# Another cut of the tokens for a fused linear attention and gated MLP: nine tokens of a head per partition, pairs of heads in 64-row halves

## The chip, the cores and the metric

The kernel runs on one core of a Trainium2 chip. The metric is device microseconds of one execution; the time before is the median of three runs. The engines are TensorE (PE, with the weight loads as a row of their own, PEld), VectorE (DVE), ScalarE (ACT), GpSimd (POOL) and SyncE (SP), which here only issues DMAs and waits. PSUM has 8 banks of 512 float32 a partition; every matmul writes there.

## The reference

Inputs: `q`, `k`, `v` of shape (8 batches, 8 heads, 576 tokens, 64), `w_phi` (64 x 128), and for the MLP `w_val`, `w_out` (512 x 512) and `conv_w` (5 x 512), all float32.

```python
def phi(x):
    proj = np.einsum('bhsd,df->bhsf', x, w_phi)
    proj = proj - np.max(np.abs(proj), axis=-1, keepdims=True)
    return np.concatenate([np.exp(proj), np.exp(-proj)], axis=-1)
q_p, k_p = (phi(q), phi(k))
kv = np.einsum('bhsf,bhsd->bhfd', k_p, v)
z = np.sum(k_p, axis=2)
num = np.einsum('bhsf,bhfd->bhsd', q_p, kv)
den = np.einsum('bhsf,bhf->bhs', q_p, z)[..., None] + 1e-06
attn = num / den                      # heads side by side: x of (8, 576, 512)

gate_pre = sum over k of conv_w[k] * (x shifted down by 4 - k tokens, zeros ahead)
out = (sigmoid(gate_pre) * (x @ w_val)) @ w_out
```

So every token and head needs two projections to 128 features, the largest magnitude of each, and 256 exponentials for q and for k. The sum over tokens KV (with a column of ones for z) must be complete for a head before any of its outputs can be computed. The convolution looks at a token and the four before it.

## The kernel before

**Units.** The 576 tokens of a head are cut into 512 main tokens, four neighbours on each of 128 partitions, and a tail of 64. A main unit is one pair of heads of one batch (32 of them); a tail unit holds the tails of two batches, all heads (4). 36 units in all.

**One unit's steps**, by the names in the list and the lines of the profile:
- `T` (L331): four transposes each for k and q, 128x128, into one bank; `Tc` copies that bank to SBUF (L224 on DVE, L222 on ACT).
- `PK`, `PQA` (L342): projection of k and q with tokens on the output partitions, eight matmuls of 64 rows each, for the two halves of the rows into two banks. `mKa`, `mK`, `mQa`, `mQ` (L356) take the largest magnitude of each, one bank at a time.
- `E` (L382) and `K0` to `K3` (L388): exponentials on ACT. The maximum of k is not subtracted; its exponential scales v instead, in `V` (L408, on POOL), whose extra column (L412) carries the scale for z.
- `PQ` (L466): projection of q again, now with features on the partitions, two matmuls of 64 rows by 512 columns. `SH` (L476) subtracts the maximum in PSUM, with a broadcast column against a negated identity, eight matmuls of 128 rows and columns. `Qa`, `Q` (L484): exponentials, 512 elements at a time.
- `KV` (L445, L450): 16 matmuls of 128 rows for the main tokens and 4 for the tail; `KVM` copies the sums to SBUF (L224, L222). `NUM` (L509; L523 for tails), then `XN`: reciprocal (L534) and product (L536).
- `XP`: a DMA transpose issued by SP (L545, L548) puts the normalised tokens, channels on partitions, into `XT` (tails: `XH`).

**The MLP**, for each batch: `GA` (L604) computes the convolution with diagonal 64x64 weights, four tiles of the array at a time, in two calls of 32 matmuls with two banks each; `TH` (L612) the tanh; `VAa`, `VAb` (L617) the product with `w_val`; `GV` (L633) gate times value; `OUT` (L642) the product with `w_out`; `OE` (L649 on ACT, L651 on DVE) the evacuation with a factor of one half; `ST` (L663) the store. `GAt`, `THt`, `GVt`, `OUTt` (L673 to L712) do the same for the tails of two batches.

**Loads.** `LD` (L295) issues them, most from POOL, which converts float32 to bfloat16 on the way; a main load takes rows of 1,024 bytes, a tail's rows of 256.

**Order.** Nothing is scheduled at run time. The string `ORDER` lists every step with its PSUM bank (`@`) and, where there is a choice, its engine (`:D`, `:A`, `:P`); each engine and queue executes its own steps in the order of the list, and waits for semaphores. So a step that waits holds all that stands behind it on the same engine.

A matmul addresses a part of the array: 128 rows, or a half of 64, and the same for columns. Matmuls in different parts can overlap.

Of the kernel before, what the change touches and what calls it, by code (L numbers as in the profile page):

```python
# [2 lines left out]

# [7 lines left out]
ALU = mybir.AluOpType  # L11
# [9 lines left out]
SM = 512  # L21
ST = S - SM
E1 = D + 1
PL = 144
TL = 80
NG = B // 2
NU = 9 * NG


# [7 lines left out]
LD5 V2:P mKa4 K33 K04 KVM1:D NUM1@4 PQ3@6,3 SH3 mK4 XN1 LD11 K13 KV2@2 K24 LD31 PQA4@7,4 KVM2:D E3
mQa4 K14 mQ4 PQ0@1,5 K34 SH0 LD30 Qa3 Qa0 NUM2@6 PQ4@2,0 T5@4 T6@1 Q3 SH4 Q0 XN2 Qa4 E4 Tc5:D
Tc6:D PK5@7,6 mKa5 K05 PQA5@3,1 PK6@2,5 mQa5 Q4 LD13 K15 mK5 LD12 V3:P K25 KV3@3 mQ5 V4:P mKa6 K06
LC0 K35 KVM3:D E5 V5:P LD32 LD39 PQ5@0,1 TP0@7 mK6 Vb0:P NUM3@3 CW0 XP1 XN3 K16 XP2 T7@7 Tc7:D K26  # L40
SH5 Qa5 PQA6@6,2 mQa6 PK7@3,7 mKa7 KV4@4 PQA7@6,0 mQ6 mQa7 XP3 K36 T8@5 Tc8:D mK7 PQ6@2,6 Q5
KVM4:A SH6 K07 NUM4@4 mQ7 XN4 E6 PK8@0,1 K17 mKa8 Qa6 K27 T9@2 Tc9:D Q6 XP4 PQA8@3,5 V6:P PQ7@4,6
SH7 mQa8 LD15 mK8 K08 K37 PQA9@2,3 mQ8 mQa9 KV5@7 KVM5:D mQ9 T10@5 Tc10:D K18 PQ8@0,2 SH8 Qa7
PK9@4,7 mKa9 T11@3 E7 V7:P Q7 PK10@5,6 Tc11:D K28 mKa10 LD14 DG0:P Qa8 K38 KV6@3 Q8 K09 NUM5@0 mK9
KVM6:D NUM6@2 XN5 K010 mK10 KV7@0 K29 K110 XN6 K19 KVM7:D T12@5 PK11@1,4 mKa11 K210 HL0:P Tc12:D
XP6 LD16 K39 GA0@2 K310 mK11 K011 NUM7@6 VAa1@0 LD40 XN7 E8 VAb1 TH0 GV1 V8:P PK12@2,5 PQA10@3,6
K111 PQ9@1,7 SH9 VAa2@0 K211 mQa10 mKa12 LD19 VAa0@3 mK12 E9 LD17 K311 Qa9 VAb0 mQ10 KV8@4 KVM8:D
VAb2 GV0 PQA11@1,6 K012 V9:P Q9 mQa11 K212 PQ10@4,7 SH10 mQ11 K112 T13@3 Tc13:D NUM8@1 XN8 E10
# [59 lines left out]
def kernel(  # L110
# [653 lines left out]
```

## Time and profile before

| | |
|---|---|
| runs | 235.14, 232.63, 233.62 us; median 233.62 |
| profiled execution, first to last instruction | 232.5 us (the page gives no other time for it) |
| busy, PE / PEld | 205.8 us (89%) / 139.5 us (60%) |
| busy, DVE / ACT / POOL | 184.2 (79%) / 188.6 (81%) / 125.4 us (54%) |
| chain that ended last, by engine | PE 69%, ACT 11%, DMA 9%, DVE 5% |
| mean granted clock of TensorE | 0.972 |
| maxima L356 / exponentials L388 and L484, calls | 144 / 288 |

A line of groups reads: source line, engine, operation, output<-inputs with shapes, count, then busy time and the mean of one, then idle time of the engine before them. A line of the timeline begins with the start and the length in us, and ends with an idle time where the engine waited. A line of stages gives the window, its length, busy time and count of PE, PEld, DVE, ACT and POOL, the granted clock, and the DMA's share and rate. A PE duration holds some latency: the next matmul starts before it ends.

### The profile page before, as it was taken

How to read it: one execution, taken by the hardware profiler on the slowest of the kernel's cores; microseconds unless marked ns; L12 is line 12 of the kernel's file. 1: busy time of each engine (PE TensorE's matmuls, PEld its weight loads, DVE VectorE, ACT ScalarE, POOL GpSimd, SP SyncE). 2: the span in 40 equal slices, each digit the busy share in tenths (PEclk: the TensorE clock that was granted, in tenths of full speed). 3: DMA queues.
4: the chain of work that ended last, by engine and by line, in shares of the span. 5: the costliest groups of instructions: out<-in, count | busy, mean ns of one | idle time of the engine just before them, and what ended most of it. 6: DMA issues, size and time to landing. Idle time of an engine off the chain costs nothing.

```text
span 232.5 us, 8372 instructions
## 1 busy us (share of the span) xinstructions
PE 205.8 (89%) x3497; PEld 139.5 (60%) x3516; DVE 184.2 (79%) x335; ACT 188.6 (81%) x419; POOL 125.4 (54%) x142
## 2 busy tenths in 40 slices
PE   1286797888999989899999999999899999999991
PEld 1264675666666746567666766766476667564550
DVE  5559669999989979699999879897799788554451
ACT  3189869999997988599999979998899999934251
POOL 8909935999979437774919751564526241100000
PEclk9998579999999999999999999999999999999997
DMA  8997995979999942999994992499903928126195
GB/s 151 246 198 97 106 180 80 92 101 178 129 194 128 139 32 32 129 257 177 128 114 68 180 186 92 39 115 126 214 6 37 169 77 259 38 52 200 27 355 185
DMA packets 62002, 30.90 MB, mean 133 GB/s; under 512 B 33420, under 2 KB 59148, under 8 KB 61964
## 3 DMA queue, kind: packets, MB, share of 16 engines
q0 software_dynamic: 36144, 14.29, 58.2%
q1 hardware_dynamic: 25468, 15.78, 33.6%
q8 instruction: 27, 0.44, 0.8%
q10 hardware_dynamic: 352, 0.30, 0.4%
q14 instruction: 11, 0.09, 0.2%
HBM read 30.48 MB, written 9.44 MB: 172 GB/s over the span
## 4 chain that ended last, share of the span: by engine, by line
PE 69%; ACT 11%; DMA 9%; DVE 5%; issue 3%; SPq 1%; POOL 1%; POOLq 0%; DVEq 0%; ACTq 0%
PE PS L617 11%; PE PS L642 10%; PE PS L342 7%; PE PS L604 7%; PE PS L476 7%; PE PS L445 6%; PE PS L331 6%; DMA XT<-XN 6%; PE PS L509 5%; ACT QTIL L484 5%; ACT KTIL L388 3%; DMA kT<-in_k_dram 3%; PE PS L466 3%; PE PS L681 2%; DVE MQ L356 2%
## 5 line engine op out<-in xcount | busy, mean ns | idle before, releaser
L408 POOL TENSOR_TENSOR VT<-vN,E 128x1024 bf16<-128x1024 bf16 x27 | 51.5, 1907 | 60.4 <-issue 34.2
L388 ACT ACTIVATE KTIL<-PS 128x512 bf16<-128x512 f32 x128 | 76.7, 666 | 5.3 <-DVE MK L356 5.1
L484 ACT ACTIVATE QTIL<-PS 128x512 bf16<-128x512 f32 x128 | 71.0, 666 | 2.5 <-PE PS L476 1.1
L356 DVE TENSOR_REDUCE MK<-PS 128x4 f32<-128x512 f32 x72 | 47.9, 683 | 7.5 <-PE PS L342 7.2
L356 DVE TENSOR_REDUCE MQ<-PS 128x4 bf16<-128x512 f32 x72 | 47.4, 683 | 1.3 <-PE PS L342 1.2
L342 PE MATMUL PS<-W,T 64*128 64x128 bf16 x576 | 29.6, 227 | 5.8 <-DVE T L224 1.9
L617 PE MATMUL PS<-XT,WVAL 128*128 128x512 bf16 x128 | 33.8, 380 | 0.3 <-DMA XT<-XN 0.3
L342 PEld LDWEIGHTS <-T 64*128 64x128 bf16 x576 | 18.3, 98 | 21.8 <-issue 11.9
L642 PE MATMUL PS<-WOUT,GV 128*128 128x512 bf16 x111 | 29.9, 380 | 1.2 <-issue 0.5
L633 DVE SCALAR_TENSOR_TENSOR GV<-GATE,PS 128x512 bf16<-128x512 bf16 x32 | 21.6, 681 | 5.9 <-ACT GATE L612 3.1
L445 PE MATMUL PS<-VT,KTIL 128*128 128x65 bf16 x512 | 25.4, 198 | 0.8 <-DVE T L224 0.6
L536 DVE TENSOR_TENSOR XN<-PS,RCP 128x512 bf16<-128x512 f32 x36 | 24.9, 691 | 1.2
L445 PEld LDWEIGHTS <-KTIL 128*128 128x128 bf16 x512 | 22.8, 100 | 3.7 <-DVE T L224 0.8
L476 PE MATMUL PS<-nident,MQ 128*128 128x128 bf16 x288 | 23.9, 229 | 0.5 <-issue 0.5
L612 ACT ACTIVATE GATE<-PS 128x1024 bf16<-128x1024 f32 x16 | 16.7, 1044 | 8.8 <-PE PS L604 8.7
L476 PEld LDWEIGHTS <-MQ 128*128 128x128 bf16 x288 | 17.6, 102 | 9.5 <-issue 8.8
L224 DVE COPY T<-PS 128x1024 bf16<-128x1024 bf16 x31 | 21.1, 684 | 2.7 <-PE PS L331 2.3
L509 PEld LDWEIGHTS <-QTIL 128*128 128x128 bf16 x512 | 19.3, 99 | 5.5 <-DVE KVS L224 1.1
L509 PE MATMUL PS<-KVS,QTIL 128*128 128x65 bf16 x512 | 21.4, 196 | 1.3 <-DVE KVS L224 0.8
L450 PE MATMUL PS<-VZ,KTt 128*128 128x65 bf16 x128 | 21.9, 196 | 0.0
L604 PE MATMUL PS<-XT,DIAG 64*64 64x384 bf16 (+3 forms) x512 | 20.6, 299 | 1.0 <-issue 0.8
L642 PEld LDWEIGHTS <-GV 128*128 128x128 bf16 x128 | 11.3, 98 | 12.4 <-issue 0.6
(73 smaller groups left out, 304.1 us busy)
## 6 DMA issues: line engine op xcount, KB each, us to landing
out_dram<-OS SPq DMA_DIRECT2D x14, 512.0 KB, 3.8
kN<-in_k_dram POOLq DMA_DIRECT2D x7, 512.0 KB, 9.0
qN<-in_q_dram POOLq DMA_DIRECT2D x7, 512.0 KB, 8.4
vN<-in_v_dram POOLq DMA_DIRECT2D x7, 512.0 KB, 6.9
vF<-in_v_dram SPq DMA_DIRECT2D x2, 512.0 KB, 7.6
out_dram<-OSt SPq DMA_DIRECT2D x8, 128.0 KB, 2.4
out_dram<-OS SPq DMA_DIRECT2D x4, 256.0 KB, 2.9
qT<-in_q_dram POOLq DMA_DIRECT2D x8, 64.0 KB, 5.2
```

The costliest lines, as they stand in the source:

```text
L342: nc.tensor.matmul(PS[:, bank[rg], blk * P:(blk + 1) * P], u.T[r, i, blk, :], W2[r, :], start=True, stop=True,)
L356: nc.vector.tensor_reduce(dst, PS[:, bank, :].rearrange("p (b f) -> p b f", f=F), AX.X, ALU.max, apply_absolute_value=True,)
L388: nc.scalar.activation(u.KT[:, ft, rg, :, :].rearrange("p b f -> p (b f)"), PS[:, u.PK[rg], :], AF.Exp, scale=1.0 if ft == 0 else -1.0,)
L408: eng.tensor_tensor(dst[:, :, :, 0:D], x.unsqueeze(1).to_broadcast([n, 2, 8, D]), e.unsqueeze(3).to_broadcast([n, 2, 8, D]), ALU.mult,)
L445: nc.tensor.matmul(o, u.KT[:, ft, rg, h2 * 2 + j2, :], u.VT[:, ft, (h2 * 2 + j2) * 2 + rg, :], start=(c == 0), stop=False,)
L476: nc.tensor.matmul(PS[:, u.PQ[rg], blk * P:(blk + 1) * P], u.MQ[:, rg, blk:blk + 1].to_broadcast([P, P]), nident[:, :], start=False, stop= ...
L484: nc.scalar.activation(u.QT[:, ft, rg, :, :].rearrange("p b t -> p (b t)"), PS[:, u.PQ[rg], :], AF.Exp, scale=1.0 if ft == 0 else -1.0,)
L509: nc.tensor.matmul(ps[:, j2, x * E1:(x + 1) * E1], u.QT[:, ft, rg, h2 * 2 + j2, :], u.KVS[:, (ft * 2 + h2) * E1:(ft * 2 + h2 + 1) * E1], s ...
L536: nc.vector.tensor_tensor(u.XN[:, :, :, :], nv[:, :, :, 0:D], RCP[:, :, :].unsqueeze(3).to_broadcast([P, 2, 4, D]), ALU.mult,)
L604: nc.tensor.matmul(ps[c, par, j0 * P:j1 * P], DIAG[r, dt, 4 - dl, :], mv, start=(i == 0), stop=(i == len(parts) - 1), skip_group_check=True,)
L617: nc.tensor.matmul(PS[:, m.val[jt], :], WVAL[:, dt, jt * P:(jt + 1) * P], XTs[m.b % 2][:, dt, :, 16:PL], start=(dt == 0), stop=(dt == 3),)
L642: nc.tensor.matmul(PS[:, bank[0], :], m.GV[:, jt, j * P:(j + 1) * P], WOUT[:, jt, :], start=(jt == 0), stop=(jt == 3),)
```

## The change

The kernel is written anew around another cut of the tokens, with another list.

- A partition holds nine neighbouring tokens of one head; 64 partitions hold a head, 128 a pair. Plane n is the n-th token of every partition. A unit is a pair of heads with planes 0 to 7 (32 units); plane 8 of a batch's four pairs makes a "halo" unit, one per batch (8). In the list, units have plain names (`T5`, `KV5`), halos a trailing e (`Te1`, `PKe1`).
- The two heads of a pair lie on different halves of the partitions, so transposes, `SH` and `KV` become 64-row matmuls, one half for each head: 16, 16 and 36 a unit, where there were 8, 8 and 20. T's output and the KV sums take two banks each.
- `mQ` takes the maximum over two banks in one call; `Qp`, `Qm` are exponentials over two banks. K stays with one bank a call.
- `PQ` is split. Both halves of the rows write both banks, so `PQb` may start only when `PQa` has finished: `WQ` puts a nop on SP that waits for `PQa`'s last matmul, and `PQb`'s first matmul waits for that nop.
- Taps: 32x32 diagonal weights, 16 tiles of the array, 144 matmuls a batch into four banks; plane 8 of two batches is computed together by `GAe`, 80 matmuls, `VAe`, `OUTe`.
- `w_val` is loaded in its own order and rearranged by four POOL copies (`WC`); `w_out` in four loads.
- Loads take rows of 2,304 bytes. The second to fourth unit to be started belong to batch 1, whose k and q are loaded whole (`LQ1`, `LK1`).
- 28 of the 32 units reach `XT` by the DMA transpose on SP (`XC` without an engine), the last four, and the halos, by PE transposes. A store is two DMAs, for even and odd planes.
- Eight matmuls of zeros stand ahead of everything on PE.

```diff
-SM = 512
-ST = S - SM
+HP = H // 2
+NPL = 9
...
+    for i in range(NF):
+        nc.tensor.matmul(PS[:, 7, :], zero[:, 0:P], zero[:, :], start=True, stop=True)
...
     def op_T(i, bank):
         u = units[i]
-        u.Tps = PS[:, bank[0], :].bitcast(BF16).rearrange("p (i b t) -> p i b t", i=2, b=4)
+        u.Tps = half(bank[0], 256).bitcast(BF16)
         for n, name in enumerate(("k", "q")):
-            for blk in range(4):
-                nc.tensor.transpose(u.Tps[:, n, blk, :], col(u, name, blk), ident_bf[:, :])
+            for jj in range(4):
+                for h2 in range(2):
+                    r = row(h2)
+                    nc.tensor.transpose(
+                        u.Tps[:, h2, (n * 4 + jj) * 64:(n * 4 + jj) * 64 + 64],
+                        tok(name, u.b)[r, u.hp, jj * P:(jj + 1) * P], ident[r, r],
+                    )
 
     def op_Tc(i, eng):
         u = units[i]
-        u.T = ktp.tile([P, 2, 4, P], BF16, name="T")
-        copy(eng, u.T[:, :, :, :], u.Tps)
+        u.T = ktp.tile([P, 2, 4, 2, 64], BF16, name="T")
+        copy(
+            eng, u.T[:, :, :, :, :].rearrange("p n j h t -> p h (n j) t"),
+            u.Tps.rearrange("p h (x t) -> p h x t", t=64),
+        )
...
+    def op_mQ(i):
+        u = units[i]
+        u.MQ = maxp.tile([P, 2, 4], BF16, name="MQ")
+        absmax(u.MQ[:, :, :], half(u.PQA, 512).rearrange("p g (j f) -> p g j f", f=F))
...
+    def op_KV(i, bank):
+        u, t = units[i], halos[units[i].b]
+        u.KVps = half(bank[0], 2 * E1)
+        for ft in range(2):
+            for n in range(NPL):
+                for h2 in range(2):
+                    r = row(h2)
+                    if n < 8:
+                        kt, vt = u.KT[r, ft, n % 2, n // 2, :], u.VT[r, ft, n, :]
+                    else:
+                        kt, vt = t.KT[r, ft, u.hp % 2, u.hp // 2, :], t.VT[r, ft, u.hp, :]
+                    (nc.tensor.matmul(
+                        u.KVps[:, h2, ft * E1:(ft + 1) * E1], kt, vt,
+                        start=(n == 0), stop=(n == 8), skip_group_check=True,
+                    ))
...
+    def unswapped(proj, u):
+        u.last = [proj(u, g, 1) for g in range(2)][1]
...
+    def relay(u):
+        u.relay = nc.sync.nop()
+        behind(u.relay, u.last)
+
+    def swapped(proj, u):
+        behind([proj(u, g, 0) for g in range(2)][0], u.relay)
+
+    def featproj(u, g, swap):
+        h2 = g ^ swap
+        return nc.tensor.matmul(
+            PS[:, u.PQ + h2, :].rearrange("p (j g t) -> p g j t", g=2, t=64)[:, g, :, :],
+            W2[row(g), :], u.T[row(g), 1, :, h2, :],
+            start=True, stop=False, skip_group_check=True,
+        )
...
+    def submax(bank, cols):
+        for n, col in enumerate(cols):
+            for h2 in range(2):
+                r = row(h2)
+                nc.tensor.matmul(
+                    PS[:, bank + h2, n * 64:n * 64 + 64], col[r, :].to_broadcast([64, P]), nident[r, r],
+                    start=False, stop=True, skip_group_check=True,
+                )
...
+    def qexp(u, ft):
+        new_qt(u)
+        nc.scalar.activation(
+            u.QT[:, ft, :, :, :].rearrange("p h n t -> p h (n t)"), half(u.PQ, 512),
+            AF.Exp, scale=1.0 if ft == 0 else -1.0,
+        )
...
+    def taps(X, bank, rs, parts):
         for i, (dl, j0, j1) in enumerate(parts):
-            for dt, r, c, par in quarters(q2):
+            for dt in range(4):
+                for r in rs:
+                    rr = slice(32 * r, 32 * r + 32)
+                    g = PS[32 * dt:32 * dt + 32, bank[r // 2] + r % 2, j0 * 64:j1 * 64]
...
+                    nc.tensor.matmul(
+                        g, DIAG[rr, dt, 4 - dl, :], mv,
+                        start=(i == 0), stop=(i == len(parts) - 1), skip_group_check=True,
+                        tile_position=(32 * r, 32 * dt),
+                    )
```

Two lines of the new list, from the middle, and one from its end:

```
Tc15:D mKb14 XCe2:D KV13@0 Ka14 E14 OE1_1:D PQb13 SH13 PQA14@2 KVM13:A LV4 GA2@0,4 mQ14 NUM12@2 RCP12 V14:P
Qm13 Qp13 XN12 NUM13@6 THx2 PQa14@0 WQ14 T16@2 RCP13 PQb14 XN13 SH14 Tc16:D THy2 PK15@4,5 KV14@6 mKa15 XC12
...
OUT7_1 OE7_1:A STe2 ST6_3 VAe3@7 OUT7_2 OUTp7_3@2 THey3 OUT7_3 ST7_0 GVe3 OUTe3@3 OE7_2:A ST7_1 OEe3:A OE7_3:D
```

More of the change, by code (lines that the diff above doesn't have):

```diff
@@ L37 @@
[L37 to L42, printed above, removed]
@@ L456, in op_KVM @@
     def op_KVM(i, eng):
         u = units[i]
[L458 to L469 removed]
+        u.KVS = kvp.tile([P, 2, 2 * E1], BF16, name="KVS")
```

986 lines of the change are left out of this document (534 added, 452 removed), and 14 rows, old and new, of the table LOADS.

## The prediction

> **What bounds the kernel now.** I read the busy time by stage first, then short stretches of the timeline, where the distance from the start of one group to the start of the next gives what an operation occupies of its engine (a duration also holds latency that the next operation overlaps).
>
> ```profile
> 45.00:195.00 150.00, 143.51 (x2629) 98.44 (x2644) 134.24 (x245) 138.82 (x313) 92.01 (x98) 1.00 0.99 125
> 195.00:228.00 33.00, 32.01 (x446) 18.30 (x448) 17.25 (x33) 17.11 (x33) 2.10 (x2) 1.00 0.48 149
> 8.05 0.60 ACT L388 ACTIVATE KTIL<-PS 128x512 bf16<-128x512 f32 x1 [2.62 <-DVE MK L356]
> 203.26 1.13 ACT L484 ACTIVATE QTIL<-PS 128x512 bf16<-128x512 f32 x2
> 227.76 0.69 DVE OS L651
> ```
>
> The stage rows give PE, PEld, DVE, ACT and POOL in that order. From 45 to 195 us PE is busy 143.5 of 150 (96%), ACT 138.8, DVE 134.2: PE binds, with two engines close behind. From 195 to 228 PE is full and the others half idle: MLP work left over when attention has ended. ACT's exponentials run from 8.05 to 204.4; the last evacuation starts at 227.76 and ends at 228.5, and the store with the closing takes 4 more to 232.5. So time falls with PE work, but only until ACT or DVE binds.
>
> **PE's work, before and after.** What each block occupies:
>
> ```profile
> 103.06 1.29 PE L604 MATMUL PS<-XT,DIAG 64*64 64x512 bf16 x32
> 104.29 0.40 PE L342 MATMUL PS<-W,T 64*128 64x128 bf16 x8
> ...
> 105.29 0.29 PE L445 MATMUL PS<-VT,KTIL 128*128 128x65 bf16 x4
> ...
> 105.92 0.66 PE L509 MATMUL PS<-KVS,QTIL 128*128 128x65 bf16 x16
> 106.41 1.03 PE L617 MATMUL PS<-XT,WVAL 128*128 128x512 bf16 x4
> ...
> 109.61 0.40 PE L342 MATMUL PS<-W,T 64*128 64x128 bf16 x8
> 109.85 0.38 PE L466 MATMUL PS<-T,W 64*128 64x512 bf16 x2
> 110.06 0.39 PE L342 MATMUL PS<-W,T 64*128 64x128 bf16 x8
> 110.38 0.62 PE L476 MATMUL PS<-nident,MQ 128*128 128x128 bf16 x8
> 110.84 1.03 PE L617 MATMUL PS<-XT,WVAL 128*128 128x512 bf16 x4
> 111.70 0.29 PE L445 MATMUL PS<-VT,KTIL 128*128 128x65 bf16 x4
> ```
>
> A unit before: KV, 20 matmuls, 105.92-105.29 = 0.63; NUM 0.49; projections PK and PQA 0.24 each (109.61 to 109.85); PQ 0.21; the maximum subtraction SH 0.46 (8 of 128 columns), and the 8 transposes T, of the same shape, 0.45. L342 takes 0.32 where the next group has another tile shape, so a change of shape costs about 0.09. Taps GA: 1.23 with a change, 1.13 without, twice a batch; a VA block 0.86, and OUT, of the same shape, as much. Sums: 32 main units of 2.72 = 87.0; 4 tails of 2.1 = 8.5; MLP 8 x (2.26+3.44+3.44) = 73.1; the tails' MLP 4 x 2.3 = 9.2; 164 changes of shape (counted along the matmul rows) x 0.09 = 14.8. Together 193.
>
> After, T (16 matmuls), SH (16) and KV (36) have 64 rows and 64 or 65 columns, in alternating halves of the array, a form that this trace lacks. The nearest rows:
>
> ```profile
> 96.35 0.76 PE L673 MATMUL PS<-XH,DIAG 64*64 64x128 bf16 x40
> 97.05 1.07 PE L681 MATMUL PS<-XH,WVAL 128*128 128x128 bf16 x16
> 118.54 0.70 PE L523 MATMUL PS<-KVS,QTt 128*64 128x65 bf16 x32
> ```
>
> L673, four tiles at once: (0.70-0.09)/40 = 15 ns each. L523, two halves by columns, 65 wide: 0.70, less the 0.17 by which L509's 0.66 exceeds its 0.49, over 32 = 16 ns. L509, one tile, 65 wide: 0.49/16 = 31. So 15 to 31 ns; I take 16, since L342 (two row halves, 128 wide: 0.24/8 = 30 ns, half of L476's 57) shows row halves running side by side with full-width weights. Then T is 0.26 for 0.45, SH 0.26 for 0.46, KV 0.58 for 0.63: 0.44 less a unit, 14 in all; at 31 ns it would be 0.58 more a unit, 19 in all.
>
> The Trainium skill, "TensorE: Matmul & The Clock Gate", section "Back-to-back issue gap", speaks against this: a matmul of 1 to 64 columns still takes about 60 cycles, a floor of 25 ns. By that floor 68 matmuls would take 1.7 us a unit and 144 taps 3.6 us a batch, an estimate that undoes the gain. The 15 and 16 ns of L673 and L523 disagree, at least where neighbours use different tiles.
>
> The rest of PE: PK, PQA, PQ and NUM keep columns and concurrency, 1.18, so a unit is 2.28, x32 = 73.0. Eight halos of 1.1 (Te 0.26, PKe 0.24, PQe 0.11, SHe 0.13, NUMe 0.26, XPe 0.11) = 8.9. Four units' PE transposes XP at the end 0.9. Taps in 32x32 tiles, also unseen: 16 tiles at once halve the columns, 2.26 to 1.13, if the array limits; 144 x 15 ns = 2.2 if each costs L673's pace. I take 1.5, nearer the array's, since most of the 144 are long. MLP 8 x 8.4 = 67.0. The halos' MLP has 80 taps, 0.3 to 1.2, taken 0.7: 4 x 2.5 = 9.8. Changes of shape, counted in the new list, 158: 14.2. Together 174, from 166 to 219 with the bounds.
>
> **The relays.** In 40 places PQb now waits for an SP nop that itself waits for PQa's last matmul; all that stands behind PQb on PE waits along, and DVE and ACT for that.
>
> ```profile
> 5.30 0.61 PE L331 MATMUL PS<-ident_bf,qN 128*128 128x128 bf16 x4
> 5.94 0.69 DVE L224 COPY T<-PS 128x1024 bf16<-128x1024 bf16 x1
> 6.69 1.04 PE L342 MATMUL PS<-W,T 64*128 64x128 bf16 x16 [0.79 <-DVE T L224]
> L545 SPq DMA_TRANSPOSE XT<-XN x32: 1189/1210/2460, 28.4 to 208.9; - x32
> ```
>
> PE's end at 5.91 starts DVE at 5.94, DVE's end at 6.63 starts PE at 6.69: hops of 0.03 and 0.06. The latency of a 256-column matmul is about 0.28 (L466's 0.38 less half of the 0.21 it occupies). PE must then cover 0.37 less the 0.11 that PQa occupies, 0.26. The list puts a PE block of 0.23 to 0.9 between in most places, some 0.12 in four, nothing in four: about 3 us. On SP a relay also queues behind crossbar transposes, which wait for XN and hold SP 1.21 us each; seven stand within six entries ahead of a relay, four of these well covered: 2 us. I take 5 (no gain is possible; 25 at 0.6 a relay). PE after: 179, which is 14 less.
>
> **ACT and DVE.**
>
> ```profile
> 46.17 1.89 ACT L388 ACTIVATE KTIL<-PS 128x512 bf16<-128x512 f32 x3
> 47.60 1.43 ACT L484 ACTIVATE QTIL<-PS 128x512 bf16<-128x512 f32 x2
> 48.56 0.66 ACT L382 ACTIVATE E<-MK 128x8 f32<-128x8 f32 x2
> 48.76 1.44 ACT L484 ACTIVATE QTIL<-PS 128x512 bf16<-128x512 f32 x2
> 200.65 1.02 ACT L612 ACTIVATE GATE<-PS 128x1024 bf16<-128x1024 f32 x1 [0.58 <-PE PS L604]
> 201.56 1.08 ACT L484 ACTIVATE QTIL<-PS 128x512 bf16<-128x512 f32 x2
> 203.00 0.42 ACT L222 ACTIVATE KVS<-PS 128x260 bf16<-128x260 f32 x1
> 60.07 1.28 DVE L356 TENSOR_REDUCE MK<-PS 128x4 f32<-128x512 f32 x2
> 61.27 0.68 DVE L356 TENSOR_REDUCE MQ<-PS 128x4 bf16<-128x512 f32 x1
> 62.16 0.43 DVE L224 CAST KVS<-PS 128x260 bf16<-128x260 f32 x1 [0.22 <-PE PS L450]
> 62.51 0.68 DVE L633 SCALAR_TENSOR_TENSOR GV<-GATE,PS 128x512 bf16<-128x512 bf16 x1
> 64.30 0.68 DVE L224 COPY T<-PS 128x1024 bf16<-128x1024 bf16 x1
> 64.90 0.20 DVE L534 RECIPROCAL RCP<-PS 128x8 f32<-128x8 f32 x1
> 65.14 0.69 DVE L536 TENSOR_TENSOR XN<-PS,RCP 128x512 bf16<-128x512 f32 x1
> ```
>
> ACT: 512 elements occupy 1.43/3 = 0.477, a pair E 0.20, 1024 elements 0.91, a KVS copy 0.26. Up to its last exponential it does 288 exponentials (137), 36 E pairs (7), 13 tanh and 5 T copies (16), and 24 smaller ones (12): 172 in the 196 from 8.05, 88%. The change: pairing Q's exponentials over two banks saves 0.04 each, 64 times (-2.8); four T copies go (-3.7); eight KVS copies come (+2.1); four output evacuations, a tanh and eight halo E pairs more fall before the last exponential (+4). It stays at 172.
>
> DVE: a 512 maximum or T copy occupies 0.60, a KVS copy 0.35, RCP with XN 0.24 + 0.61. 144 maxima 86, T 19, KVS 8, XN 31, GV 21, OS 10, start 4: 179. Q's merged maximum of 1024 occupies about 1.11 (0.60, plus 512 at the 1 ns that an element costs between 260 and 512), 32 of these save 3: 176. The T copy now goes in runs of 64 elements; I leave it at 0.60; at one element per ns it would be 1.1 (+19).
>
> Loads come in 2,304-byte rows for 1,024 and 256, but the second unit now needs two whole-batch loads. I cost the start at nothing, 3 us either way; it is hidden by unit 0 as before. The 8 warm-up matmuls lie ahead of the first transpose, where PE idles; uncovered, 8 of L617's 0.22 or twice that. The weight copies go to POOL (92 of 150 busy), uncovered about 4.
>
> **The sum.** Up to its last exponential ACT, with 172, is then fullest; PE has 179-18 = 161 there, DVE some 166. PE was 96% busy where it bound; I give ACT 94%: 172/0.94 = 183 from 8 us on, to 191. Behind the last exponential the list has some 18 of PE work (taps, VA and OUT of batch 7, three OUT of batch 6, two halo groups), then 1 of waits, 0.7 evacuation and 4 of closing: 23.5, where before it was 28. End 214.5; the profiled execution spans 232.5 and the median of the runs is 233.6, so I add 1: 215.
>
> **Rivals.**
> - PE stays the bound: relays of 0.3 on the mean (12), taps at 2.0 (+4) make 190 of PE, 3 less than before, and the end is 4.5 shorter: 226 (222 to 231). For it: T, KV and taps now take twice the PSUM banks, so PE waits more for others to empty them. Against: most relays are covered.
> - Slower: the halves cannot load weights side by side, so 64-row matmuls go at L509's 31 ns: 68 x 15 ns x 32 = 33, PE 212, 19 above before, less 4.5: 248. It decides from 22 ns a matmul, where PE is back at 193. For it: no 128-wide weights go under 30 ns here. Against: L342's halves.
> - A floor for every small matmul, taps too, at L509's 31 ns: 33 more for units, 5 for halos, 144 x 31 = 4.5 a batch of taps (+24) and 7 for the halos' taps: PE 248, time about 284. L673 and L523 speak against it. The page cited above would set this floor at 25 ns.
> - The T copy loses its rate: DVE 195, 186 of it to its last maximum; at 94% 198 + 8, and 26 behind it: 233, no change.
> - The list packs ACT at 98%: 176 + 8 + 23.5 + 1 = 208 or a little less.
>
> **Chances.** Forecast 0.57 (own range 208 to 222), packed better 0.08, PE-bound 0.17, T copy 0.06, slower by loads or by relays above 0.5 each 0.10, floor 0.02. Range for 8 in 10: 204 to 231; it leaves out the slower cases and most of the T copy's. 1% is about what a measurement of this kernel can tell from no change: faster by more (under 231.3) 0.81, within it 0.07, slower 0.12.
>
> **What would show it.** Right: KV in 64-row groups at 0.58, ACT fullest with few gaps, PE under 90% in the middle, an end of some 20 us with PE alone full. Wrong: KV near 1.1, PE waits for SP above 10 us in all, T copies over 1 us, or ACT gaps that end with PE.

## The result, and the profile after

The changed kernel takes 267.6 us (median of four executions, 265.51 to 274.22), the kernel before 233.88 us. The ratio is 1.143, with a 95% interval of 1.135 to 1.151. Ratios and their intervals leave out executions more than 1.5% above the fastest of their kernel; e1, e3 and h1 below have only one execution within it, so for them the median and the lowest of all are given. The profiled execution spans 265.7 us, where 215 had been predicted and 231 was the end of the range.

The page of the changed kernel: busy time, the slices of PE and of the granted clock, the queue that carries instructions, and the shares of the chain that ended last.

```profile
PE 208.1 (78%) x5596; PEld 140.4 (53%) x5596; DVE 179.1 (67%) x307; ACT 188.7 (71%) x377; POOL 101.9 (38%) x124
...
PE   5367875958946999497976787689988998799791
...
PEclk9995799797997999779999999599999999799997
...
q8 instruction: 43, 0.70, 1.1%
...
PE 51%; DVE 15%; issue 13%; ACT 11%; DMA 7%; POOL 1%; DVEq 0%; POOLq 0%; SPq 0%; ACTq 0%
```

No engine works longer than before by more than 2.3 us (PE 205.8 before, ACT 188.6, DVE 184.2). Of the 33 us by which the profiled execution is longer, 32 are more idle time of PE, and "issue" has 13% of the chain where it had 3%. The stages of the changed kernel, in the columns of the stage rows before:

```profile
45.00:195.00 150.00, 120.06 (x3285) 80.77 (x3285) 107.67 (x185) 110.77 (x224) 59.97 (x72) 0.92 0.60 102
195.00:240.70 45.70, 40.60 (x1249) 26.98 (x1239) 30.42 (x56) 34.59 (x69) 15.70 (x16) 0.96 0.41 90
240.70:265.70 25.00, 17.92 (x345) 10.33 (x342) 9.33 (x17) 7.19 (x13) 0.00 (x0) 0.94 0.51 125
```

In the middle PE is busy for 80%, ACT for 74% and DVE for 72%; before it was 96, 93 and 89%. Nothing is full. What PE waits for, in the view of waits (total us, times, longest):

```profile
PE PS L723 <- issue: 12.3, 5, 3.8
PE PS L434 <- issue: 6.7, 3, 2.5
PE PS L723 <- DMA XT<-XN: 4.0, 1, 4.0
PE PS L788 <- issue: 3.3, 1, 3.3
PE PS L303 <- DMA kN<-in_k_dram: 2.6, 1, 2.6
PE PS L319 <- issue: 2.3, 1, 2.3
```

"Issue" means that no semaphore released PE: its operands were there. All such stretches come to 26.5 us; in the kernel before they are 1.7 (3.0 with the gaps that missing records leave; see the table below). The timeline of PE around one of them:

```profile
103.59 0.43 PE L434 MATMUL PS<-VT,KT 64*128 64x65 bf16 x16
103.86 0.19 PE L434 MATMUL PS<-VTe,KTe 64*128 64x65 bf16 x2
103.89 0.42 PE L434 MATMUL PS<-VT,KT 64*128 64x65 bf16 x16
104.15 0.19 PE L434 MATMUL PS<-VTe,KTe 64*128 64x65 bf16 x2
104.18 0.27 PE L469 MATMUL PS<-T,W 64*128 64x256 bf16 x2
104.29 0.40 PE L487 MATMUL PS<-nident,MQ 64*128 64x64 bf16 x16
104.52 0.39 PE L319 MATMUL PS<-W,T 64*128 64x128 bf16 x8
104.86 1.47 PE L723 MATMUL PS<-XT,DIAG 32*32 32x512 bf16 x100
110.01 0.84 PE L723 MATMUL PS<-XT,DIAG 32*32 32x189 bf16 x44 [3.68 <-issue]
```

KV takes 0.59 for its 36 matmuls and SH 0.23 for 16, as forecast. Then PE stops 3.7 us in the middle of 144 taps that depend on nothing new. Counting PE's instructions (a matmul and its weight load are two) in the order of the trace, each of the twelve such stretches, 0.2 to 3.8 us long, begins at the 193rd of 256. A block of 256 instructions is what one packet of q8 holds: 16,384 bytes, 64 each. There are 43 such packets, where the kernel before had 27; it has 7,032 PE instructions, the changed kernel 11,192. PE resumes 1.3 to 1.5 us after a packet of q8 has landed, every time. PE runs out of instructions.

### The profile page after: what moved, and what is told of

Same layout as the page of the kernel before. It is cut to its first block, busy times and chain, and to the rows that moved or that the text cites. A ratio compares the mean times of both kernels' runs of the same rounds, so it can differ in the third digit from the quotient of the medians.

```text
span 265.7 us, 12474 instructions
## 1 busy us (share of the span) xinstructions
PE 208.1 (78%) x5596; PEld 140.4 (53%) x5596; DVE 179.1 (67%) x307; ACT 188.7 (71%) x377; POOL 101.9 (38%) x124
## 4 chain that ended last, share of the span: by engine, by line
PE 51%; DVE 15%; issue 13%; ACT 11%; DMA 7%; POOL 1%; DVEq 0%; POOLq 0%; SPq 0%; ACTq 0%
PE PS L788 8%; PE PS L759 7%; PE PS L434 7%; PE PS L723 6%; ACT KT L384 5%; PE PS L520 5%; DVE MK L336 5%; DVE MQ L336 4%; DMA kN<-in_k_dram 4%; PE PS L319 4%; DMA XT<-XN 4%; PE PS L303 3%; PE PS L469 2%; ACT QT L502 2%; DVE XN L538 2%
## 5 line engine op out<-in xcount | busy, mean ns | idle before, releaser
L384 ACT ACTIVATE KT<-PS 128x512 bf16<-128x512 f32 x128 | 68.3, 637 | 12.4 <-DVE MK L336 8.8
L502 ACT ACTIVATE QT<-PS 128x1024 bf16<-128x1024 f32 x64 | 63.5, 1053 | 5.8 <-PE PS L487 5.8
L336 DVE TENSOR_REDUCE MQ<-PS 128x8 bf16<-128x1024 f32 x32 | 39.0, 1219 | 11.4 <-PE PS L319 11.0
L748 ACT ACTIVATE GATE<-PS 128x1024 bf16<-128x1024 f32 x16 | 15.6, 1022 | 23.7 <-PE PS L723 23.7
L434 PE MATMUL PS<-VT,KT 64*128 64x65 bf16 x1024 | 25.1, 198 | 8.6 <-issue 6.7
L723 PE MATMUL PS<-XT,DIAG 32*32 32x384 bf16 (+8 forms) x1152 | 17.5, 304 | 16.4 <-issue 12.3
L434 PEld LDWEIGHTS <-KT 64*128 64x128 bf16 x1024 | 21.8, 99 | 10.7 <-issue 7.6
L319 PEld LDWEIGHTS <-T 64*128 64x128 bf16 x512 | 18.9, 102 | 14.4 <-issue 12.2
L520 PE MATMUL PS<-KVS,QT 128*128 128x65 bf16 x512 | 22.7, 200 | 2.1 <-ACT QT L502 0.9
L723 PEld LDWEIGHTS <-DIAG 32*32 32x32 bf16 x1152 | 12.6, 89 | 20.9 <-issue 19.0
L520 PEld LDWEIGHTS <-QT 128*128 128x128 bf16 x512 | 19.8, 102 | 5.0 <-ACT QT L502 1.3
L469 PE MATMUL PS<-T,W 64*128 64x256 bf16 x128 | 19.4, 294 | 1.8 <-DVE MQ L336 0.5
L759 PEld LDWEIGHTS <-WVAL 128*128 128x128 bf16 x128 | 11.7, 102 | 15.8 <-issue 4.9
```

Source lines behind the costliest of these rows:

```text
L319: (nc.tensor.matmul(PS[:, banks[g], jj * F:(jj + 1) * F], T[row(g), n, jj, :, :].rearrange("p h t -> p (h t)"), W2[row(g), :], start=True, ...
L336: nc.vector.tensor_reduce(dst, x, AX.X, ALU.max, apply_absolute_value=True)
L384: nc.scalar.activation(u.KT[:, ft, par, :, :].rearrange("p b f -> p (b f)"), PS[:, u.PK[par], :], AF.Exp, scale=1.0 if ft == 0 else -1.0,)
L434: (nc.tensor.matmul(u.KVps[:, h2, ft * E1:(ft + 1) * E1], kt, vt, start=(n == 0), stop=(n == 8), skip_group_check=True,))
L469: return nc.tensor.matmul(PS[:, u.PQ + h2, :].rearrange("p (j g t) -> p g j t", g=2, t=64)[:, g, :, :], W2[row(g), :], u.T[row(g), 1, :, h ...
L502: nc.scalar.activation(u.QT[:, ft, :, :, :].rearrange("p h n t -> p h (n t)"), half(u.PQ, 512), AF.Exp, scale=1.0 if ft == 0 else -1.0,)
```

## The experiments

Sums of the profiled executions, for reference below. "Idle" is the span less PE's busy time, "no semaphore" the part of it put down to issue, "half clock" PE's busy time inside stretches with a granted clock of 0.5, "work" the busy time less half of that. Span = work + half of "half clock" + idle. PE instructions are twice the weight loads of the trace; the texts written before the runs count five fewer for each kernel.

Two things are allowed for in the table. The profiles of before, e1, e2 and e3 lack 19, 34, 29 and 19 records of matmuls, and each leaves a gap of 0.05 to 0.18 us that looks idle without a semaphore; these gaps, 1.3, 2.9, 2.2 and 1.3 us in all, are counted as work. And the record of the clock begins late, at 18.2 us in before, 16.9 in after, 17.6 in e3 and 4.6 to 5.5 in the others. PE was at half speed ahead of it: two groups of eight transposes of the changed kernel start 0.21 us apart there, and 0.13 later at full clock. This time is counted as half clock.

```profile
13.49 0.40 PE L303 MATMUL PS<-ident,kN 64*128 64x64 bf16 x8 [2.58 <-DMA kN<-in_k_dram]
13.70 0.40 PE L303 MATMUL PS<-ident,qN 64*128 64x64 bf16 x8
...
64.64 0.29 PE L303 MATMUL PS<-ident,kN 64*128 64x64 bf16 x8
64.77 0.28 PE L303 MATMUL PS<-ident,qN 64*128 64x64 bf16 x8
```

| kernel | PE instructions | span | idle | no semaphore | half clock | work |
|---|---|---|---|---|---|---|
| before | 7,032 | 232.5 | 25.4 | 1.7 | 17.1 | 198.6 |
| after | 11,192 | 265.7 | 57.6 | 26.5 | 42.3 | 186.9 |
| e1, 64x64 taps | 9,720 | 244.4 | 38.6 | 5.2 | 30.0 | 190.7 |
| e2, full rows | 8,472 | 248.1 | 31.0 | 1.2 | 22.7 | 205.8 |
| e3, before, taps split | 8,056 | 242.6 | 30.8 | 6.9 | 26.7 | 198.4 |
| g1, after, few loads | 11,192 | 240.2 | 41.1 | 12.3 | 20.5 | 188.8 |
| f3, e1 with later loads | 9,720 | 238.4 | 37.2 | 6.2 | 18.2 | 192.1 |

So against the kernel before the change gives 11.7 us of work and takes 32.2 of idle time (24.8 of it without a semaphore) and 12.6 through the clock: some 33 together. This divides the time and is no proof of what each part costs. The column of work is good to 1 or 2 us: kernels with the same matmuls (after and g1, e1 and f3) differ by as much.

### First set: instructions, array or relays

Theory A: the supply of PE instructions. Rivals: B, the small tiles are slow in the array; C, the relays and what hangs on them.

**e1_taps64**, the changed kernel with the taps of the kernel before:

```diff
-    DIAG = const.tile([P, 4, 5, 32], BF16, name="DIAG")
+    DIAG = const.tile([P, 4, 5, 64], BF16, name="DIAG")
...
-                for r in rs:
-                    rr = slice(32 * r, 32 * r + 32)
-                    g = PS[32 * dt:32 * dt + 32, bank[r // 2] + r % 2, j0 * 64:j1 * 64]
+                for r2 in range(2):
+                    rr = row(r2)
+                    g = PS[row(dt % 2), bank[dt // 2] + r2, j0 * 64:j1 * 64]
```

> The changed kernel with its taps in 64x64 tiles (72 matmuls a batch and 40 for two halos, where it has 144 and 80); channels permuted to suit, nothing else changed. PE instructions 11187 -> 9715. Theory A (PE runs out of instructions: they come in blocks of 256, and a block that is used up in under some 4 us leaves PE idle until the next one is there): the taps themselves take 0.7 us more a batch (+6), but most idle stretches that end without a releaser inside and behind the taps go (8 of 13, some 18 us, and the cold clock behind them): 250 us, between 244 and 257. Theory B (the work in the array sets the time, small tiles as such are slow or not): 32x32 taps busy 17.5 us in all, so +6: 272. Theory C (relays over SP hold PE): relays are all there, no gain: 267 to 273.

Measured: 246.9 us median, within A and far from B and C. Single executions of this variant lie from 238.8 to 249.0, the lowest being below A's range; against the lowest of the changed kernel (265.5) the gain is 26.8 us, by the medians 20.7. Half the tiles with twice the columns cost PE some 4 us of work (190.7 against 186.9; 6 were expected), and the time without a semaphore falls from 26.5 to 5.2 us. What is left of the waits:

```profile
PE PS L303 <- DMA kN<-in_k_dram: 5.1, 1, 5.1
PE PS L723 <- DMA XT<-XN: 4.7, 1, 4.7
PE PS L434 <- issue: 2.8, 3, 1.7
PE PS L319 <- issue: 1.7, 1, 1.7
```

**e2_hybrid**, e1 with transposes of 128 rows and query features laid out by plane instead of by head, so that SH has 128 rows again and the relays go; q's exponentials are one bank a call again:

```diff
-                    nc.tensor.transpose(
-                        u.Tps[:, h2, (n * 4 + jj) * 64:(n * 4 + jj) * 64 + 64],
-                        tok(name, u.b)[r, u.hp, jj * P:(jj + 1) * P], ident[r, r],
-                    )
+                nc.tensor.transpose(
+                    u.Tps[:, x * P:(x + 1) * P], tok(name, u.b)[:, u.hp, jj * P:(jj + 1) * P], ident[:, :],
+                )
...
-        swapped(featproj, units[i])
+        pass
```

> The changed kernel with 64x64 taps, with 8 transposes of 128 rows for T (one bank) in place of 16, and with PQ and SH cut by plane parity instead of by head: two matmuls of 512 columns and eight of 128 rows, so that no bank is written by two row halves and all 40 relays go; the exponentials of q are one bank a call again. KV stays in 64-row halves. PE instructions 11187 -> 8467. Work in the array rises by about 0.2 (T) + 0.2 (SH) a unit and 0.7 a batch of taps: +19. Theory A: the idle stretches without a releaser fall to a few us, 236 us (228 to 245). Theory B: 280 or more. Theory C: the relays' part goes but the array's 19 come: 260 to 280.

Measured: 249.5 us, ratio 1.070 (1.060 to 1.080): outside all three ranges and so a miss for A, though only 1.2 us are now without a semaphore. A's number left out the other side of the exchange. On the timeline of e2 four transposes stand 0.22 apart and eight SH matmuls, with a change of shape, take 0.54:

```profile
104.19 0.38 PE L302 MATMUL PS<-ident,kN 128*128 128x128 bf16 x4 [0.19 <-DVE XN L540]
104.41 0.39 PE L302 MATMUL PS<-ident,qN 128*128 128x128 bf16 x4
104.64 0.61 PE L484 MATMUL PS<-nident,MQ 128*128 128x128 bf16 x8
105.18 0.40 PE L314 MATMUL PS<-W,T 64*128 64x128 bf16 x8
```

With whole rows T takes 0.45 a unit, where 64-row halves need 0.24: work 205.8 instead of 190.7. ACT is busy for 194.2 us instead of 189.0. Fewer instructions were bought with more work. The relays are gone and nothing was gained, which speaks against C; their waits on SP sum to 0.4 us in the changed kernel.

**e3_split**, the kernel before with each tap matmul cut into two of half the columns:

```diff
-                nc.tensor.matmul(
-                    ps[c, par, j0 * P:j1 * P], DIAG[r, dt, 4 - dl, :], mv,
+                for x in range(2):
+                    nc.tensor.matmul(
+                        ps[c, par, j0 * P:j1 * P].rearrange("p (j t) -> p j t", t=P)[:, :, 64 * x:64 * x + 64],
+                        DIAG[r, dt, 4 - dl, :], mv[:, :, 64 * x:64 * x + 64],
```

> The kernel before, with every tap matmul cut into two of half its columns (64 to 256 columns each): same tiles, same columns in all, same list, 1024 more PE instructions (7027 -> 8051), all of them in the taps. Theory A: the taps now use up 128 instructions in 1.1 us, so idle stretches without a releaser appear at block ends in and behind them, some 5 to 10 of 1 to 3 us: 241 us (236 to 249). Theory B and C: the columns are the same and 0.0 to 0.2 us a call come from pace: 233 to 236.

Measured: 244.9 us, within A; the kernel before took 235.3 on that chip. The lowest of each are 240.4 and 231.6. Work is the same (198.4), and stretches appear that the kernel before does not have:

```profile
PE PS L342 <- issue: 2.3, 1, 2.3
PE PS L605 <- issue: 2.0, 1, 2.0
```

This is the cause without any other part of the change: the same columns, the same layout, 1,024 more instructions, and 9.6 us by the medians. In the profiles, 10.1 us apart, 5.2 of them are idle time without a semaphore and 4.8 are charged to the clock.

**e4_probe**, the kernel before with 1,024 small matmuls behind everything:

```diff
+    def op_PR(i, bank):
+        for n in range(256):
+            for rg in range(2):
+                for cg in range(2):
+                    r = slice(rg * 64, rg * 64 + 64)
+                    nc.tensor.matmul(
+                        PS[cg * 64:cg * 64 + 64, bank[rg], 0:P], DIAG[r, 0, 4, :], XTs[1][r, 0, 0, 16:PL],
+                        start=True, stop=True, skip_group_check=True,
+                    )
```

> The kernel before with 1024 matmuls added at its end, four 64x64 tiles in turn, 128 columns each, as its halo taps (which go at 13 to 15 ns each in runs of 40); they write PSUM banks that are no longer used. 2048 instructions, 8 blocks. Theory A: one block of 256 instructions every 3.6 to 4.5 us, with an idle stretch of about 2 us after each 128 matmuls: 29 to 36 us for the run, span about 258 us. Theory B: 13 to 15 ns each throughout, 14 to 16 us, span about 242 us.

Measured: 256.8 us, span 255.0. The timeline of PE at the end:

```profile
226.49 2.37 PE L723 MATMUL PS<-XT,DIAG 64*64 64x128 bf16 x155
230.59 1.98 PE L723 MATMUL PS<-XT,DIAG 64*64 64x128 bf16 x128 [1.73 <-issue]
234.04 1.98 PE L723 MATMUL PS<-XT,DIAG 64*64 64x128 bf16 x128 [1.47 <-issue]
237.50 1.98 PE L723 MATMUL PS<-XT,DIAG 64*64 64x128 bf16 x128 [1.47 <-issue]
```

As A said: a block of 128 matmuls and their weight loads is 1.98 us of work and comes every 3.45 us, 13.5 ns an instruction, a little faster than the 3.6 to 4.5 expected. The last two blocks take 4.00, which is not explained. The Trainium skill, "Runtime: NRT & Kernel Launch", section "Instruction fetch mechanics", describes this mechanism: blocks of 16 KiB or 256 instructions, and the next one is fetched on the sequencer's own DMA queue while the current one executes. The block size agrees with the packets here. It adds that the fetch is mostly hidden; here it is hidden only where a block lasts longer than 3.45 us, and that with the DMA engines idle.

### Second set: what e1 still loses

Theory D: the waits for loads and transfers that are left, and the half clock behind them. Rival E: the list as a whole no longer fits.

**f1_ramp**: other order of the first loads. **f2_warm**: zero matmuls ahead of the first transposes of batch 1. **f3_xbar**: two loads later. **f4_ramp_xbar**: f1 and f3.

```diff
-Kb0 LQ1 LKa0 PQb0 SH0 Qp0 LK1 Qm0 LQa0 T4@4 mKa0
+Kb0 LKc1 LQc1 PQb0 SH0 Qp0 LKd1 LQd1 Qm0 LKa0 LQa0 T4@4 mKa0
...
-Qm0 LQa0 T4@4 mKa0
+Qm0 LQa0 WM12@4 T4@4 mKa0
...
-VA4_1@7 LK7 THx4 THy4 mQ22 Te6@4 PQA23@0 LV6 Tce6:D
-LQ7 GV4_1
+VA4_1@7 THx4 THy4 mQ22 Te6@4 PQA23@0 LV6 Tce6:D
+GV4_1
...
-mQ24 V23:P Qm23 Ee6
+mQ24 V23:P LK7 LQ7 Qm23 Ee6
```

> The changed kernel with 64x64 taps (the run e1_taps64, 246.9 us) and another order of the first loads: the first plane of batch 1's keys and queries ahead of its other planes, and batch 1's values behind batch 0's keys and queries. Theory D (what the 64x64 variant still has above the kernel before is PE idle time, and the half clock that each idle stretch brings with it; in that run PE was idle 5.1 us for the keys of batch 1 and the clock was 0.5 from 8.9 to 32.8 us): the wait for the keys falls under 1.5 us, the stretch at half clock gets at least 7 us shorter, time 240 us (236 to 243). Rival E (the list as a whole no longer fits the durations, and what one wait gives back the next ones take): 245 to 249 us.

> The 64x64 variant with 12 matmuls of 512 columns on the zero tile put ahead of the first transposes of batch 1, where PE is idle 5.1 us for the keys; nothing else is moved. Theory D: at half clock 12 x 0.43 = 5.2 us, so they fit into the wait; if idleness is what lowers the clock, the stretch at half clock (8.9 to 32.8 us) gets 5 to 15 us shorter and the time falls by half of that, to 242 us (239 to 245). Rival E: the clock's stretch may get shorter, but the time stays at 245 to 249 us. If idleness does not lower the clock: the same stretch, 246 to 249 us.

> The 64x64 variant with the loads of batch 7's keys and queries issued some 10 us later, behind the value products of unit 23, so that they do not run beside the transposing transfers for which the taps of group 4 wait. Theory D: the wait at 154.8 us (4.7 us of PE) falls under 1.5 us, the half-clock stretch of 6.8 us behind it goes, time 241 us (239 to 244). Rival E: 245 to 249 us, with the same microseconds idle at a later place.

> Both reorderings of loads together on the 64x64 variant. Theory D: the two gains add, 235 us (231 to 239), with PE idle time of 41.5 us in the profile falling to some 33 us. Rival E: 243 to 249 us.

Measured: f1 242.7, f2 248.1, f3 238.0, f4 238.1 us; the ratios to the kernel before are 1.040, 1.065, 1.020 and 1.024 (f4: 1.018 to 1.029). f1 is within D, at its end: it removes the wait for the keys, but 2.0 us of it come back as a wait for ACT to leave the bank, and its stretch at half clock is only 3.4 us shorter (20.5). f3 does as D said, and is a little faster than D's range: the wait for the transfer falls to 1.4 us. f4 is within D's range and below E's, and its idle time falls to 32.6 us as D said; but it is no faster than f3 alone, so the two gains do not add, as E said of such gains. Neither theory is met as a whole. f2 has E's time, but was no test: its matmuls waited for the same bank and came behind the wait, not into it.

```profile
10.99 0.61 PE L491 MATMUL PS<-nident,MQ 64*128 64x64 bf16 x16 [0.54 <-DVE MQ L340]
13.63 1.87 PE L298 MATMUL PS<-zero 128*128 128x512 bf16 x4 [2.03 <-ACT QT L506]
```

### Third set: why a block comes late

The stretches of the changed kernel, up to 3.8 us, are longer than a fixed 3.45 us a block allows. The trace shows when each packet of q8 starts. Two windows, each from the moment PE enters a block to the start of the packet that it will need next:

```profile
55.60:58.55 2.95, 1.69 (x131) 1.36 (x129) 1.24 (x3) 1.09 (x2) 0.00 (x0) 1.00 1.20 197
61.10:62.15 1.05, 1.05 (x35) 0.83 (x36) 0.09 (x1) 0.67 (x1) 0.00 (x0) 0.56 0.00 0
```

With the DMA engines full (share 1.20, 197 GB/s; the share adds up the times of all packets and can pass 1) the packet started 2.95 us after PE had entered the block; with the DMA engines empty, 1.1 us after. Over all 43 packets of the changed kernel the median is 1.10 us where the DMA share was up to 0.8, and 2.47 where it was higher, with single ones from 0.5 to 4.5. Hence theory W: the refill waits behind data.

**g1_after_fewloads** and its control **g2_before_fewloads** leave out the loads of keys, queries and values of batches 3 to 7 (the edit shown is g1's):

```diff
+        b = min(b, 2)
         if (name, b) not in toks:
...
     def load(eng, name, b, p0, p1):
+        if b > 2:
+            return
```

> The changed kernel with the loads of keys, queries and values of batches 3 to 7 left out; those batches compute on batch 2's data, every instruction of PE, DVE and ACT stays. Theory W (a block of 256 PE instructions is refilled only once PE has entered the block before, and the refill waits behind the data that the 16 DMA engines are carrying: in the changed kernel's trace it starts 1.0 to 1.15 us after PE enters a block where the DMA engines are idle and 1.9 to 4.5 us after where they are full): with fewer loads PE idles without a semaphore for 6 to 10 us instead of 26.5, its waits for the transposing transfers go too (4 us), and the half clock behind those stretches shrinks; time 240 us (232 to 248). Rival A0 (the refill has a fixed pace of 13.5 ns per instruction, whatever else moves): the idle time without a semaphore stays at 20 to 26 us, time 256 to 266 us, the gain being only the waits for transfers.

> The same loads (and the tails of the last two groups) left out of the kernel before: the control for the run above. Both theories: it idles without a semaphore for 3.0 us and for transfers for 4.1 us, most of that ahead of batch 3, so 228 to 234 us. A gain of over 8 us here would mean that the loads hold the kernels back in another way than through the refill.

Measured: g1 240.6 us (236.9 to 243.2), g2 230.4 us, the kernel before 234.0 on that chip. The same loads are worth 27 us to the changed kernel and 3.6 to the kernel before. W's time is met (240), its idle time not quite: 12.3 us without a semaphore, where 6 to 10 were expected and A0 expected 20 to 26. No instruction of PE was taken away. Its waits:

```profile
PE PS L306 <- DMA kN<-in_k_dram: 4.8, 1, 4.8
PE PS L726 <- issue: 3.7, 3, 1.6
PE PS L437 <- issue: 3.2, 3, 1.4
```

The middle of the changed kernel and of g1, in the columns of the stage rows:

```profile
45.00:210.00 165.00, 132.90 (x3773) 89.99 (x3774) 117.02 (x201) 122.01 (x248) 67.38 (x80) 0.93 0.59 101
45.00:210.00 165.00, 147.45 (x4429) 99.85 (x4423) 135.17 (x235) 142.96 (x291) 65.78 (x73) 0.99 0.30 61
```

The wait at the taps for the transposing transfer (4.0 us) is gone too, and the clock in the middle is 0.99, so not all of the 27 us is refill: of the idle time 14.2 us less is without a semaphore, and half of the 21.8 us less at half clock is 10.9, if that time was paid in full.

**g3_probe_busy**, e4 with loads beside its matmuls:

```diff
     def op_PR(i, bank):
+        for n in range(4):
+            for name in ("k", "q", "v"):
+                t = (loadv if name == "v" else loadp).tile([P, H, 4 * D], BF16, name=name + "N")
+                if n == 0:
+                    nc.gpsimd.tensor_copy(t[:, 0, 0:8], batches[7].GV[:, 2, 0:8])
+                nc.gpsimd.dma_start(t[:, :, :], main_src(name, n, 0, H))
```

> The probe run (the kernel before with 1,024 small matmuls at its end: a block of 256 instructions every 3.45 us) with twelve loads of a batch's keys, queries or values (7 MB written, some 30 us of transfers) beside those matmuls. Theory W: while the loads run, a refill starts 2 to 4.5 us after PE enters a block, so a block takes 4.5 to 7 us, and the time is 264 to 280 us (256.8 without the loads). Rival A0: 3.45 to 4.0 us a block, 256 to 260 us.

Measured: 273.4 us, within W. The rows of the timeline that answer to those of e4:

```profile
234.29 3.46 PE L729 MATMUL PS<-XT,DIAG 64*64 64x128 bf16 x128 [4.64 <-issue]
240.48 3.34 PE L729 MATMUL PS<-XT,DIAG 64*64 64x128 bf16 x128 [2.74 <-issue]
246.68 2.76 PE L729 MATMUL PS<-XT,DIAG 64*64 64x128 bf16 x128 [2.86 <-issue]
...
269.00 1.61 PE L729 MATMUL PS<-XT,DIAG 64*64 64x128 bf16 x101 [0.39 <-issue]
```

And the stage, with the DMA share as the last but one column:

```profile
234.30:265.30 31.00, 16.84 (x644) 15.89 (x645) 0.00 (x0) 0.00 (x0) 3.44 (x4) 0.61 1.37 191
```

A block comes every 6.20 us while the loads run, and 3.73 us after they have ended. In the 6.20 a packet starts 3.75 us after PE has entered a block, takes 0.96, and PE goes on 1.45 later; in e4 the same three are 1.1, 1.0 and 1.3. The clock was at half for much of it, so PE's own part is longer than in e4, but the packet's start, not PE, sets the distance. A0 falls, W stands.

**g4_spread**, f3 with the loads of keys and queries of batches 3 to 6 in pieces, such as:

```diff
-LK3
+LKp3_0
...
+LKp3_1 LKp3_2
```

> The 64x64 variant with the later loads of batch 7 (the run f3_xbar, 238.0 us), and the loads of keys and queries of batches 3 to 6 issued as four loads of one plane each, one or two behind each of the following value products on POOL. Theory W: a refill then finds fewer bytes ahead of it, so the idle time without a semaphore falls from 6.2 us to 2 to 4, time 236 us (233 to 239). Rival A0: no change of that idle time, 237 to 240 us. In both, if a plane comes late for its transposes, PE waits for it and the time is above 240 us.

Measured: 252.9 us, ratio 1.081 (1.072 to 1.090), slower than both ranges, as foretold for planes that come late. The time without a semaphore falls from 6.2 to 2.3 us, as W expected, but the last pieces of the queries come too late for the halos' transposes, and those waits cost more than the refill did:

```profile
PE PS L581 <- DMA qN<-in_q_dram: 10.7, 5, 3.7
```

### Fourth set: e1 and f3 side by side, and the start

**h1_taps64_again** and **h2_xbar_again** are e1 and f3 unchanged. **h3_warm_free_bank** and **h4_other_bank** are f4 with:

```diff
-LKa0 LQa0 T4@4 mKa0
+LKa0 LQa0 WM5@6 T4@4 mKa0
...
-LKa0 LQa0 T4@4 mKa0
+LKa0 LQa0 T4@6 mKa0
...
-T5@0 Te1@6 mKb0
+T5@0 Te1@4 mKb0
```

> The 64x64 variant once more, in more executions and on the chip of the three runs beside it. Its four executions so far went from 238.8 to 249.0 us, so that the gains of later variants over it (4 to 9 us) are within its own spread. Theory D (the waits for loads and transfers are paid in full): median 244 to 249 us. Rival E2 (its three slow executions were disturbed, and it takes what the reordered variants take): median 237 to 241 us.

> The 64x64 variant with batch 7's loads of keys and queries later, once more beside the run h1_taps64_again. Theory D: 236 to 240 us, at least 5 us below the 64x64 variant. Rival E2: within 2 us of it.

> Both reorderings of loads (the run f4_ramp_xbar, 238.1 us) with five zero matmuls of 512 columns into a bank that nothing else uses then, ahead of the first transposes of batch 1, where PE idles 2.0 us for a bank. At half clock they take 5 x 0.43 = 2.1 us. Theory H (the half clock in the first 32 us costs what PE works in it, some 15 us of work at half speed): the stretch ends 5 to 15 us earlier and the time is 234 us (231 to 237). Rival: there PE waits for ACT and DVE, so a faster PE gains under 1 us: 237 to 240 us.

> Both reorderings of loads, and the first transposes of batch 1 in banks 6 and 7 instead of 4 and 5, so that they do not wait 2.0 us for ACT to read the query features of unit 0 (the halo's transposes go to banks 4 and 5 instead). Theory H: the start gets 1.5 to 3 us shorter: 235.5 us (234 to 237.5). Rival (the start is bound by the loads or by ACT): 237.5 to 240 us.

Measured: h1 244.6 (238.5 to 247.0), h2 240.3 (236.4 to 244.5), h3 241.7 (236.4 to 246.0), h4 238.0 (235.4 to 239.1); the kernel before 234.0. h1 is within D. The later loads give 4.3 us in the medians, between both expectations, and the executions overlap, so that gain is likely and not established. h3 is slower than both its ranges, and h4 is within its rival's. In h3 the zero matmuls stand in the wait, and the recorded clock was 0.79 between 8.5 and 33 us, where it was 0.52 in h4 (first row h3, then h4):

```profile
8.50:33.00 24.50, 17.75 (x409) 12.60 (x409) 20.53 (x28) 21.01 (x47) 11.49 (x14) 0.79 1.00 186
8.50:33.00 24.50, 17.70 (x390) 14.24 (x390) 20.16 (x27) 21.14 (x48) 11.01 (x14) 0.52 0.97 182
```

PE did 409 matmuls in h3, and 390 with the slow clock of h4; the five of zeros are among the 409. With the time ahead of the first record (13.4 us in h3, 4.5 in h4) PE was at half speed for some 15 us of this window in h3 and 23 in h4. That the zeros did this is not shown: two profiles of one kernel, e1 and h1, have 24 and 18. No time was gained, the profiles spanning 236.1 and 236.2 us, though only 2 us were at stake (half of PE's 23.7 us of work at half clock in h4 less 19.7 in h3). At the start ACT and DVE, busy for 21 and 20 of 24.5 us, probably set the pace, so that the half clock is covered. So the 12.6 us that the table charges to the clock is an upper bound; how much of the part behind the stretches in the middle is paid was not measured by itself.

## Why the prediction was wrong

**The step that failed** is in the sum: "PE was 96% busy where it bound; I give ACT 94%". It took PE, with 161 us of work, to be an engine that never holds the others up, and a matmul to cost only what it occupies of the array. The change halves what many matmuls occupy and doubles their number, and a term for getting those instructions to PE was missing. In its place the runs showed at least 3.45 us for 256 instructions (e4) and 6.20 beside full DMA engines (g3), and 26.5 us of PE waiting for them in the changed kernel. ACT was busy for 74% of the middle, not 94, since PE stopped in the middle of the taps and ACT waited for them, 23.7 us where it had waited 8.7 (first row the kernel before, then the changed kernel):

```profile
ACT GATE L612 <- PE PS L604: 8.7, 9, 3.5
L748 ACT ACTIVATE GATE<-PS 128x1024 bf16<-128x1024 f32 x16 | 15.6, 1022 | 23.7 <-PE PS L723 23.7
```

The last exponential ends at 240.7 (its row starts at 239.72 and lasts 1.02), not at 191. Of the prediction's signs, "PE under 90% in the middle" came true (80%) for another reason, since PE stood still; "ACT gaps that end with PE", a sign of being wrong, was the one that told.

The trace of before held the warning. It has 27 packets on q8, and there too PE idles three times without a semaphore close to the 193rd instruction of a block (at 69.24, 135.47 and 163.35), for 0.4 to 0.8 us. A block of 256 lasted some 8.6 us (232.5/27). The prediction's own paces make 144 taps of 1.5 us, 288 instructions, less than a quarter of that for more than a block.

**Point by point.**
- KV in 64-row groups at 0.58, T and SH at 0.26: right (0.59, 0.24, 0.23). The floor of 25 ns for a small matmul that the Trainium skill gives ("TensorE: Matmul & The Clock Gate", "Back-to-back issue gap") does not hold across different tiles: SH, with 64 columns, takes 0.23/16 = 14.4 ns, and KV, with 65, 0.59/36 = 16.4.
- Taps at 1.5 a batch: the shortest batch without a stop (at 246.95 us) takes 1.75 with a change of shape, 12 ns a matmul. PE's work falls by 11.7 us, with the zero matmuls at the start, 3.5 us at half clock, among the work. The sum had 193 less 174, that is 19; its "14 less" already has the relays' 5, which were to be waits.
- ACT "stays at 172", DVE 176: right in kind. Their busy times are 188.7 and 179.1, before 188.6 and 184.2. The copy of T kept its rate, 682 ns; that rival falls.
- The tail of 23.5 us behind the last exponential: 25.0.
- Relays at 5 us: 0.4 in the trace, and e2 without them is no faster.
- The start "at nothing": PE waits 2.6 us for the keys of batch 1, where it waited 3.5 us for a load before. Right here; in e1, with PE earlier, it is 5.1.
- Not in the prediction: 4.0 us of the taps waiting for a transposing transfer that ran beside three loads.
- The rivals: a slower outcome had 0.12, with halves that cannot load side by side, loads, relays or a floor as its mechanisms. None of them took place as named: the loads did cost much (g1), but through the refill. The rival "PE stays the bound" named more waiting of PE as its reason, which is nearest, but for banks, not for instructions.

**What stays open.** With 64x64 taps and the loads reordered the kernel takes 238 us, 1.6% above the kernel before (h4: 1.010 to 1.023), although PE has some 8 us less to do (work 190.8 against 198.6). In h4 only 3.0 us are without a semaphore; without the first wait of each kernel, PE waits 11.9 us for DVE and 7.9 for ACT, in many pieces, where it waited 6.3 and 3.7 before. That the list's order no longer fits its durations is the likely reason; a new list, which would show it, was not tried. No version beat the kernel before.

## What to carry to other kernels

Count PE instructions, not only columns: where many small tiles stand together, add up what the 256 instructions of a block (128 matmuls with their weight loads) occupy. In these runs PE stopped where that was less than 3.5 us, or 6 us beside heavy loads, however parallel the tiles were. A tile split that halves the array time by doubling the matmuls should pay only where longer matmuls stand between them; no run here shows one that paid. In a profile, look for "issue" at PE that returns every 256 instructions, and for packets on the instruction queue that start late.

## What the hardware showed that was not expected

- The refill of PE's instructions queues with the data: 3.45 us a block with idle DMA engines, 6.20 us with full ones, the difference being the start of one packet of 16,384 bytes, 1.1 or 3.75 us after PE enters the block before.
- Leaving out loads sped up a kernel by 27 us though PE waited for none of the data left out (its one wait for a load, 2.6 us, was for batch 1); the same loads were worth 3.6 us to a kernel with longer matmuls.
- Behind most stops of 1.8 us or more the granted clock fell to 0.5 for 3.4 or 6.8 us (at 47.6, 61.2, 81.7, 109.0, 167.0 and 228.5 us of the changed kernel), but not behind each: those at 76.1, 140.7 and 147.4, of 2.4 to 2.7 us, had none.
- Small matmuls in different tiles start every 16 ns (64 rows, 65 columns) and every 8 ns (the 80 halo taps of 32x32, 0.65 us from the first to the last start), as long as the instructions are there.
